# Moving half of a query load to ScalarE's DMA queue, and hanging the first weight loads on a sine

## Chip, cores, metric

One core of a Trainium2 chip. Its engines are TensorE (matmuls), VectorE, ScalarE (tables such as sine and Gelu), GpSimd and SyncE; the last three also issue the DMA transfers here, each into a queue of its own. "Cast" is a copy to another number type, and the granted clock is the share of its full clock that TensorE was given. L372 is line 372 of a kernel's file. The metric is the device time of one execution in microseconds (us), median over runs. All runs told here are "fast": none is over 1.5% above the fastest of its kernel. A time is some 2 us longer than the span of the profile of the same execution, which runs from the first to the last instruction.

## The reference

Linear attention with position weights, then a gated feed-forward block over the tokens. q, k and v are (8 batches, 8 heads, 576 positions, 64), all float32.

```python
theta = np.pi / 2.0 * pos / S
phi = lambda x: concat([relu(x) * cos(theta), relu(x) * sin(theta)])   # last axis
q_p, k_p = phi(q), phi(k)
kv  = einsum('bhsf,bhsd->bhfd', k_p, v);  z = sum(k_p, axis=2)
num = einsum('bhsf,bhfd->bhsd', q_p, kv); den = einsum('bhsf,bhf->bhs', q_p, z)[..., None] + 1e-6
x = (num / den) as (4608, 512)
out = (gelu(x @ w_gate) * (x @ w_val)) @ w_out                         # 512 -> 1536 -> 512
```

## The kernel before

It is already tuned: the attention of batch b+1 is spread between the feed-forward matmuls of batch b, and TensorE is rarely idle. Only the first 20 us are a bare start-up. The parts concerned (cuts marked):

```python
wg_sb = weights.tile([128, CT, J], BF16)
wv_sb = weights.tile([128, CT, J], BF16)
# ...
load(nc.sync, "k", 0, 0, 2)              # SyncE's queue, in this order: k(0) first half
load(nc.sync, "k", 0, 2, 4)              # k(0) second half
load(nc.sync, "q", 0, 0, NP, 0, JA)      # q(0), positions j 0..3
load(nc.sync, "v", 0, 0, 2)              # v(0) first half
load(nc.sync, "v", 0, 2, 4)              # v(0) second half
load(nc.sync, "q", 0, 0, NP, JA, R)      # q(0), positions j 4..8
# ... position tables on ScalarE
nc.scalar.activation(sin_t, pos_f, AF.Sin, scale=th_scale)
nc.scalar.activation(cos_t, pos_f, AF.Sin, scale=-th_scale, bias=half_pi)
warm = consts.tile([128, 1], FP32)
nc.scalar.activation(warm, half_pi, AF.Gelu)          # fetches the Gelu table early
# ...
gate = consts.tile([128, 1], FP32)
gate2 = consts.tile([128, 1], FP32)
# ... k's sines on ScalarE (and GpSimd), cosines on VectorE
prep("k", 0, 1, range(R), 2, 4, nc.scalar)            # nine sines on k's second half
# ...
nc.gpsimd.tensor_copy(gate, staged["v", 0][:, 0, 0:1])  # GpSimd waits for v(0) first half
load_w(0, 2)                                            # then issues W: w_gate and w_val, 256 columns each
load_w(2, 2)
# ...
dummies(22)                                             # matmuls that only warm TensorE's clock
sines(0, 1, 2, 3)                                       # q's sines on ScalarE
turn_j(0, 0, 2, (0, 1), 0, act_copy)                    # transposes of q on TensorE
cast_v(0, 2, 4, dve_copy)                               # VectorE casts v's second half
turn_j(0, 2, 4, (0, 1), 1, dve_copy)
kv_pairs(0, 0, 2, (6, 7))                               # the small matmuls k x v
# ...
kv_pairs(0, 2, 4, (4, 5))
# ...
prep("q", 0, 0, (4, 5))                                 # first use of q(0), positions 4..8
```

## Time and profile before

| | before |
|---|---|
| time, median | 326.56 us (3 runs); 326.49 with the three runs made later beside the changed kernel, which lie between 325.86 and 327.50 |
| profiled span | 323.9 us |
| v's second half: cast starts | 10.76 us |
| the last 32 matmuls of the first feed-forward pieces (L372) start | 19.49 us |

The prediction shows the chain and the traffic of the start.

### The profile page before, as it was taken

What the parts mean: (1) busy time and instruction counts of PE and PEld (TensorE: products, weight loads), DVE (VectorE), ACT (ScalarE), POOL (GpSimd) and SP (SyncE); (2) the same over time, 40 slices, a digit from 0 to 9 for tenths busy, and PEclk for the clock granted to TensorE, in tenths of its full rate; (3) what the DMA queues carried; (4) which work ended last, traced back from release to release, by engine and by line L of the source; (5) the groups of instructions that cost most, each with busy time, mean ns of one, the idle gap of its engine ahead of it and who ended that gap; (6) DMA issues with size and microseconds to landing.
All of it is one profiled execution on the core that took longest, in us unless ns stands there. A gap on an engine that the chain in (4) does not pass through costs nothing.

```text
span 323.9 us, 6340 instructions
## 1 busy us (share of the span) xinstructions
PE 316.8 (98%) x2451; PEld 164.5 (51%) x2451; DVE 170.3 (53%) x407; ACT 159.3 (49%) x336; POOL 26.0 (8%) x43
## 2 busy tenths in 40 slices
PE   8899999999999999999999999999999999999995
PEld 3574556555754564545544554445544444444443
DVE  5854677759665952793586348544532222222211
ACT  7864858946466832673457336633222332222220
POOL 6684410000000000000000000000000000000000
PEclk9999999999999999999999999999999999999999
DMA  7999999842999689938957990543431111111124
GB/s 274 249 186 273 297 352 366 230 111 51 323 216 354 166 147 383 201 83 251 330 96 157 383 232 1 137 102 78 85 73 33 34 32 32 35 32 32 34 65 98
DMA packets 69102, 53.57 MB, mean 165 GB/s; under 512 B 45392, under 2 KB 54352, under 8 KB 69072
## 3 DMA queue, kind: packets, MB, share of 16 engines
q1 hardware_dynamic: 59264, 41.23, 48.1%
q0 software_dynamic: 9648, 11.80, 15.7%
q8 instruction: 19, 0.31, 0.4%
q10 hardware_dynamic: 160, 0.13, 0.1%
q14 instruction: 11, 0.09, 0.1%
HBM read 37.75 MB, written 9.44 MB: 146 GB/s over the span
## 4 chain that ended last, share of the span: by engine, by line
PE 93%; DMA 2%; DVE 2%; SPq 1%; issue 0%; DVEq 0%
PE ps L400 57%; PE ps L430 28%; PE ps L282 3%; PE ps L241 3%; DMA vf<-in_v_dram 2%; PE ps L204 1%; PE ps L372 1%; PE ps L697 1%; SPq L80 1%; PE ps L357 0%; DVE qp L162 0%; DVE x_sb L322 0%; DVE vx L179 0%; DVE x_sb L295 0%; DVE qT L486 0%
## 5 line engine op out<-in xcount | busy, mean ns | idle before, releaser
L409 DVE TENSOR_TENSOR hT<-gel,ps 128x512 bf16<-128x512 f32 (+1 forms) x114 | 74.1, 650 | 128.9 <-PE ps L400 126.0
L408 ACT ACTIVATE gel<-ps 128x512 f32<-128x512 f32 (+1 forms) x114 | 64.8, 569 | 109.7 <-PE ps L400 108.0
L400 PE MATMUL ps<-xT,wv_sb 128*128 128x512 bf16 (+1 forms) x456 | 110.2, 364 | 0.0
L400 PE MATMUL ps<-xT,wg_sb 128*128 128x512 bf16 (+1 forms) x456 | 110.2, 364 | 0.0
L430 PE MATMUL ps<-wo_sb,hT 128*128 128x512 bf16 x420 | 105.8, 379 | 0.0
L400 PEld LDWEIGHTS <-wv_sb 128*128 128x128 bf16 x456 | 44.6, 98 | 47.0
L400 PEld LDWEIGHTS <-wg_sb 128*128 128x128 bf16 x456 | 44.0, 98 | 46.1
L430 PEld LDWEIGHTS <-hT 128*128 128x128 bf16 x420 | 38.3, 98 | 39.4
L439 ACT COPY o_sb<-ps 128x512 f32<-128x512 f32 x34 | 19.9, 587 | 29.9 <-PE ps L430 27.6
L160 ACT ACTIVATE qp<-qf,sin_t 128x256 bf16<-128x256 f32 x72 | 32.0, 501 | 0.4 <-DMA qf<-in_q_dram 0.4
L160 ACT ACTIVATE kp<-kf,sin_t 128x256 bf16<-128x256 f32 (+1 forms) x73 | 29.9, 479 | 0.9 <-DMA kf<-in_k_dram 0.9
L295 DVE TENSOR_TENSOR x_sb<-ps,rec 128x512 bf16<-128x512 f32 x38 | 26.3, 691 | 1.3
L162 DVE TENSOR_SCALAR qp<-qf,cos_t 128x256 bf16<-128x256 f32 x71 | 21.8, 353 | 2.3 <-DMA qf<-in_q_dram 2.3
L282 PEld LDWEIGHTS <-qT 128*128 128x128 bf16 x304 | 14.6, 98 | 7.9 <-ACT qT L486 0.3
L162 DVE TENSOR_SCALAR kp<-kf,cos_t 128x256 bf16<-128x256 f32 x63 | 18.3, 349 | 0.0
L282 PE MATMUL ps<-kv_sb,qT 128*128 128x65 bf16 x304 | 16.0, 194 | 0.0
L179 DVE CAST vx<-vf 128x1152 bf16<-128x1152 f32 (+1 forms) x15 | 12.0, 804 | 0.8 <-DMA vf<-in_v_dram 0.8
L250 ACT CAST kv_sb<-ps 128x260 bf16<-128x260 f32 x14 | 4.6, 383 | 12.9 <-PE ps L241 12.9
L241 PEld LDWEIGHTS <-kp 64*128 64x128 bf16 x504 | 8.5, 95 | 3.0 <-issue 3.0
L140 PE MATMUL ps<-dummy 128*128 128x512 bf16 x27 | 8.4, 457 | 1.5 <-POOL dummy L113 1.5
L241 PE MATMUL ps<-vx,kp 64*128 64x65 bf16 x504 | 9.3, 191 | 0.0
L294 DVE RECIPROCAL rec<-den 128x8 f32<-128x8 f32 x38 | 7.7, 203 | 1.3
(60 smaller groups left out, 100.6 us busy)
## 6 DMA issues: line engine op xcount, KB each, us to landing
out_dram<-o_sb SPq DMA_DIRECT2D x70, 128.0 KB, 2.6
kf<-in_k_dram SPq DMA_DIRECT2D x12, 576.0 KB, 6.2
vf<-in_v_dram SPq DMA_DIRECT2D x12, 576.0 KB, 8.3
qf<-in_q_dram SPq DMA_DIRECT2D x10, 576.0 KB, 5.0
qf<-in_q_dram POOLq DMA_DIRECT2D x4, 576.0 KB, 12.2
kf<-in_k_dram POOLq DMA_DIRECT2D x4, 576.0 KB, 12.5
vf<-in_v_dram POOLq DMA_DIRECT2D x4, 576.0 KB, 12.8
wg_sb<-in_moe_w_gate_dram POOLq DMA_DIRECT2D x6, 256.0 KB, 6.4
```

What stands on the lines that cost most here:

```text
L140: nc.tensor.matmul(bank(to), lhsT=dummy[:, 0:128], rhs=dummy, start=True, stop=True)
L160: nc.scalar.activation(o, i, AF.Relu, scale=tab[:, j:j + 1])
L162: (eng or nc.vector).tensor_scalar(o, i, 0.0, tab[:, j:j + 1], op0=ALU.max, op1=ALU.mult)
L179: copy(vx_tiles[b % 2][:, m0:m1, j0:j1, 0:D], staged["v", b][:, m0:m1, j0 * D:j1 * D].rearrange("p m (j d) -> p m j d", d=D),)
L241: nc.tensor.matmul(bank(6 + i)[:, m * (D + 1):(m + 1) * (D + 1)], lhsT=kp[rr, m, j, :], rhs=vx[rr, m, j, :], start=(j == 0), stop=(j == R ...
L282: nc.tensor.matmul(bank(b0 + h // 4)[:, (h % 4) * (D + 1):(h % 4 + 1) * (D + 1)], lhsT=q_cols(b, t, h), rhs=kv_sb[b][:, h // 2, h % 2, :], ...
L295: nc.vector.tensor_tensor(x, nm[:, :, :, 0:D], rec[:, :, :, None].to_broadcast([128, 2, 4, D]), op=ALU.mult,)
L400: nc.tensor.matmul(bank(b0 + g)[:, 0:w], lhsT=wt[:, ct, js], rhs=xt[:, ct, c0:c0 + w], start=(ct == 0), stop=(ct == CT - 1),)
L408: nc.scalar.activation(gel[:, 0:w], bank(b0)[:, 0:w], AF.Gelu)
L409: nc.vector.tensor_mul(hT[n][:, jt, c0:c0 + w], gel[:, 0:w], bank(b0 + 1)[:, 0:w])
L430: nc.tensor.matmul(bank(to), lhsT=hT[n][:, jt, tt * 128:(tt + 1) * 128], rhs=wo_sb[:, jt, :], start=(jt == 0), stop=(jt == JT - 1),)
L439: copy(o_sb, bank(to))
```

## The change

The intent, as far as the code tells it: SyncE's queue is relieved of its last transfer, which ScalarE issues instead, and W starts earlier. W's gate is no longer v's arrival. The sine table is written a second time into the place where W's own buffer will lie; the seventh of the nine k sines (GATE = 6) reads its factor from there, and so W's first transfer, which overwrites it, must wait for that sine and for nothing else.

```diff
+    GATE = 6
-    wg_sb = weights.tile([128, CT, J], BF16)
+    early = weights.tile([128, CT * J // 2], FP32, name="wg_sb")
 ...
-    load(nc.sync, "q", 0, 0, NP, JA, R)
 ...
     nc.scalar.activation(sin_t, pos_f, AF.Sin, scale=th_scale)
+    nc.scalar.activation(early[:, 0:R], pos_f, AF.Sin, scale=th_scale)
     nc.scalar.activation(cos_t, pos_f, AF.Sin, scale=-th_scale, bias=half_pi)
     warm = consts.tile([128, 1], FP32)
+    load(nc.scalar, "q", 0, 0, NP, JA, R)
 ...
     gate = consts.tile([128, 1], FP32)
-    gate2 = consts.tile([128, 1], FP32)
 ...
-                nc.scalar.activation(o, i, AF.Relu, scale=tab[:, j:j + 1])
+                t = early if (name, b, m0, j) == ("k", 0, 2, GATE) else tab
+                nc.scalar.activation(o, i, AF.Relu, scale=t[:, j:j + 1])
 ...
-    nc.gpsimd.tensor_copy(gate, staged["v", 0][:, 0, 0:1])
+    wg.append(weights.tile([128, CT, J], BF16, name="wg_sb"))
     load_w(0, 2)
     load_w(2, 2)
-    nc.gpsimd.tensor_copy(gate2, wg_sb[:, 0, 0:1])
+    nc.gpsimd.tensor_copy(gate, wg[0][:, 0, 0:1])
     load_w(4, 2)
-    nc.gpsimd.tensor_copy(gate2, wv_sb[:, 0, 0:1])
+    nc.gpsimd.tensor_copy(gate, wv_sb[:, 0, 0:1])
 ... (wg_sb becomes wg[0] where it is read)
```

`gate2` goes, since one small tile now serves both copies.

More of the change, by code (lines that the diff above doesn't have):

```diff
@@ L90 @@
     wo_r = moe_w_out.rearrange("(jt p) c -> p jt c", p=128)
+    wg = []
     def load_w(jt0, n):
         sl = slice(jt0 * 128, (jt0 + n) * 128)
-        nc.gpsimd.dma_start(out=wg_sb[:, :, sl], in_=wg_r[:, :, sl])
+        nc.gpsimd.dma_start(out=wg[0][:, :, sl], in_=wg_r[:, :, sl])
         nc.gpsimd.dma_start(out=wv_sb[:, :, sl], in_=wv_r[:, :, sl])
@@ L367, in gv_tile @@
     def gv_tile(t):
-        for g, wt in ((0, wg_sb), (1, wv_sb)):
+        for g, wt in ((0, wg[0]), (1, wv_sb)):
             for jt in range(2):
@@ L397, in gv_unit @@
             hT[n] = ffn.tile([128, JT, BLK], BF16, name="hT")
-        for g, wt in ((0, wg_sb), (1, wv_sb)):
+        for g, wt in ((0, wg[0]), (1, wv_sb)):
             for ct in range(CT):
```

## The prediction

> **What bounds the kernel now.** I read the page's totals first, then the chain that ended last, then the first 32 us engine by engine, and last the DMA traffic of that stretch in slices of one microsecond.
>
> ```profile
> span 323.9 us, 6340 instructions
> PE 316.8 (98%) x2451; PEld 164.5 (51%) x2451; DVE 170.3 (53%) x407; ACT 159.3 (49%) x336; POOL 26.0 (8%) x43
> PE 93%; DMA 2%; DVE 2%; SPq 1%; issue 0%; DVEq 0%
> ```
>
> TensorE carries 93% of the chain. What isn't TensorE, 7% or some 20 us, must sit where TensorE waits, and the chain of waits told in order of time says where: its first 19 us.
>
> ```profile
> 2.27 0.51 SPq L80
> 2.78 0.04 issue
> 2.82 7.92 DMA vf<-in_v_dram
> 10.74 0.02 issue
> 10.76 0.86 DVE vx L179
> 11.62 0.65 DVE qT L486 x2
> ...
> 12.48 0.29 DVE kv_sb L230
> 12.78 0.63 DVE qp L162 x2
> ...
> 13.95 1.29 DVE x_sb L322 x2
> 15.24 0.79 DVE qp L162 x2
> ...
> 19.49 1.79 PE ps L372 x32
> 21.27 6.91 PE ps L400 x32
> ```
>
> The columns are start, length, what. The second half of v(0), the fifth transfer of SyncE's queue, lands at 10.74; VectorE casts it, and from there VectorE and TensorE hand over to each other without a pause to the dense matmuls at 19.5. After that the chain is matmuls to the end, so a shift of the start is carried whole. Note that q(0)'s second part isn't on this chain: its first use is the VectorE step at 12.78, which starts when the step before it ends. It was issued at 3.39 and took 9.0 us to land (the view of that tile gives 6.1 us for the first part and 9.0 for the second), so it is there at 12.4, 0.4 us early.
>
> Why does v land at 10.74? Each slice of these lines gives busy microseconds of the engines, then granted clock, DMA share, GB/s:
>
> ```profile
> 1.00:2.00 1.00, 0.47 (x2) 0.20 (x3) 0.93 (x3) 1.00 (x1) 0.93 (x5) 1.00 0.11 21
> ...
> 4.00:5.00 1.00, 1.00 (x4) 0.38 (x3) 0.46 (x1) 0.48 (x3) 0.38 (x1) 1.00 1.05 406
> ...
> 9.00:10.00 1.00, 0.77 (x8) 0.49 (x8) 0.85 (x2) 1.00 (x4) 0.60 (x1) 1.00 1.02 393
> 10.00:11.00 1.00, 0.84 (x40) 0.76 (x40) 0.37 (x2) 0.67 (x2) 1.00 (x2) 1.00 1.07 398
> 11.00:12.00 1.00, 0.82 (x29) 0.73 (x29) 1.00 (x3) 0.69 (x2) 1.00 (x3) 1.00 0.51 169
> ```
>
> From 2 to 11 us the 16 DMA engines are full. The start is bound by bandwidth, and what counts is the order in which bytes come: k, k, q first part, v, v, and only then q second part, which is needed last. In the trace's packet records a half of k or v is 256 packets of 2304 B (16 per DMA engine, 93 ns each: 1.49 us), q's first part 512 of 1024 B (32 x 46 ns = 1.47 us), its second 512 of 1280 B (32 x 55 ns = 1.76 us). Data start at 1.95. I take 1.1 times the running sum for the slowest engine and 0.6 us to the landing, both fitted by me: 4.2, 5.8, 7.5, 9.1, 10.7, 12.7, where the trace has 4.4, 5.85, 7.9, 9.4, 10.7, 12.4.
>
> W isn't short: its first two pieces land at 14.2 (issued at 10.11, 4.1 us) and 16.5 (11.06 + 5.4), and the matmuls that read them run from 16.48 and 16.93 behind other matmuls, without an idle gap put down to a W transfer.
>
> **What the Trainium skill says.** "DMA: Bandwidth & Descriptors", section "Issuing engines are not separate DMA queues": transfers started from different engines end on the same 16 DMA engines and interleave, so issuing from a second engine saves only sequencer time. Same page, "Queues, rings and completion order": each DMA engine goes round robin over the queues that have work. The trace before agrees with the first as far as it can (one queue fills all 16 engines, share 1.02 to 1.07); it has no long overlap of two hardware queues, so the sharing itself is not yet shown here. "TensorE: Matmul & The Clock Gate", section on the warm-up: an idle window of about 3.4 us halves the clock. Before, TensorE's longest gap after the warm-up matmuls is 0.87 us and the clock row shows 9s throughout.
>
> **The change, part by part.**
> (1) It takes the sixth transfer from SyncE's queue. SyncE had issued it at 3.39 behind everything, so v is issued no earlier: gain 0.
> (2) ScalarE gets one 128x9 sine (starts are 0.12 us apart in the pair there now) and the issue (0.48 us on SyncE) ahead of the second table load. The issue starts at 2.50 + 0.12 = 2.62, the table load at 3.1 instead of 2.51, the warm Gelu ends at about 4.6 instead of 4.0, and the first k sine starts at 4.7 instead of 4.52. The wait of 0.36 us before the second half's sines swallows that: cost 0.
> (3) q's second part now flows beside k, q and v. SyncE's first data came 1.2 us after its issue began, so q's second part starts at 3.85, when three of the second k half's 16 packets are through. Packet for packet, 13 rounds of 93 + 55 ns, x1.1, are 2.1 us: that half ends at 5.97 and lands at 6.6 (5.85 before). q's remaining 19 packets pass with 19 of the first part: 19 x 101 ns x 1.1 = 2.1, to 8.1, landing at 8.7, four microseconds earlier than anyone can use it. The rest of q's first part: 13 x 46 x 1.1 = 0.66, landing at 9.35 (7.9). Then v: 11.0 (9.4) and 12.6 (10.74). The debt of 1.76 us x 1.1 has moved from the unneeded end of the queue to in front of v.
> (4) W's gate. Before, GpSimd waited for v's first half, spent 0.77 us on a copy and issued W at 10.11. Now it waits for the seventh of nine sines on the second k half. Nine took 2.74 us, so starts are 0.294 apart: 6.6 + 6 x 0.294 + 0.39 = 8.75. W is issued 1.3 us earlier. Its packets came 1.5 us after the issue and in strength after 2.4, so now at 10.3 and 11.2, in the last microsecond of v's second half. Some ten of v's 16 packets then alternate with a W packet (22.7 per engine and us in the slices where W is alone: 44 ns): +0.45 us, so v lands at 13.0.
> (5) Behind it nothing gets shorter. ScalarE's q sines run 9.35 to 11.05 (8.52 to 10.2), v's first cast ends at 11.8, the first half's 36 small matmuls and their copies are ready before 13.0. From the cast of the second half on, VectorE runs the same list. W's lead lies where TensorE doesn't wait for W.
> Sum: 13.0 - 10.74 = +2.3 us on 326.56: 328.9.
>
> **Rivals.**
> (a) v isn't delayed: the second queue's packets come later or get a smaller share, or its traffic fits beside SyncE's. For it: where W runs alone the DMA share is 1.3 to 1.46, so an engine can overlap packets. Against it: 400 GB/s in the slices already, W's own slices move no more (about 186 GB/s written, from twice as many bytes read), and q's part would have to be served behind v's, though it is issued before v's second half (2.62 against 2.82). Time then: 326 to 327.
> (b) Earlier W is worth something, or TensorE stalls on W less further on. For it: the first W pieces land only 0.4 us before their use. Against: between 19.5 and 34 us the chain is matmuls back to back. At most 0.5 us: 326.0.
> (c) TensorE cools. Its 22 warm-up matmuls end at 8.2 as before, the first transpose moves from 9.06 to about 10, and until 13.9 it is mostly idle. If the clock gate closes, the small matmuls up to the dense stage take twice their time, +1 to 2 us on top: 330 to 331. Against: no single gap reaches 3.4 us.
> (d) The packets are shared by whole transfers and not one by one: the second k half lands on time, W is issued at 8.1 and meets all of v. v lands at 13.3 to 13.7: 329.3.
>
> **Range and chances.** I give the delay (3 to 5, with d) three chances in four at 1.5 to 3 us, and a and b a quarter at -0.5 to +0.8. Weighted, the centre is a little below the sum: 328.5. Eight in ten: 326.5 to 330.3. Two per cent are 6.5 us; no part of the start that changes is long enough for a gain of that size (0.5%), and a loss would need c to come on top of everything (2%).
>
> **What would show it.** Step 3: q's second part lands near 8.7 from ScalarE's queue, q's first part after 9, v's halves near 11 and 13, with the DMA still at about 400 GB/s from 3 to 12 us. Step 4: GpSimd's first W issue at 8.1 to 8.8. Step 5: VectorE's second cast starts at 12.5 to 13.5, and the dense matmuls start about 2.3 us later than 19.49, with the spans differing by as much. Step 2: k's first sine within 0.3 us of 4.52. It is wrong if the second cast starts before 11.5; if it does start late but the dense matmuls don't, something behind the cast had slack that I didn't see. A clock row with digits below 9 in the first slices would mean c.

## More of the kernel before

One more row of the page is needed later: TensorE's granted clock, in tenths, in 40 slices of 8 us.

```profile
PEclk9999999999999999999999999999999999999999
```

## The result

The changed kernel took 329.23 us (median of 6 runs, 329.03 to 329.95), before 326.49: 1.0085 times as long, 95% interval 1.0066 to 1.0104. Every ratio here is the mean time of one kernel's fast runs over that of the other's of the same rounds, so it isn't quite the ratio of the medians. Later (experiment e6) the same changed kernel gave 328.24 and 1.0044 (1.0019 to 1.0070). So the loss is 1.3 to 2.7 us, under 1%, and how large it comes out differs between executions. The experiments show why.

The page of the changed kernel: the span and the clock row.

```profile
span 328.0 us, 6302 instructions
PEclk9789999999999999999999999999999999999999
```

The clock row, all nines before, has a 7 and an 8 in its second and third slice. Next, ScalarE's timeline (start, length, what, and in brackets the idle time before it with what ended it):

```profile
2.10 0.51 ACTq L81 DMA_DIRECT2D qf<-in_q_dram  x1
...
4.58 0.99 ACT L166 ACTIVATE kp<-kf,sin_t 128x128 bf16<-128x128 f32 x3 [0.44 <-DMA kf<-in_k_dram]
6.00 1.86 ACT L166 ACTIVATE kp<-kf,sin_t 128x128 bf16<-128x128 f32 x6 [0.43 <-DMA kf<-in_k_dram]
...
9.56 1.71 ACT L166 ACTIVATE qp<-qf,sin_t 128x256 bf16<-128x256 f32 x4 [0.83 <-DMA qf<-in_q_dram]
```

The issue goes out at 2.10, beside the sines and not behind them. k arrives almost as before (4.58 and 6.00, against 4.52 and 5.87), but the first part of q is waited for until 9.56 (8.52 before). GpSimd's and VectorE's timelines, the line of W's first issue and those of v's two casts:

```profile
8.46 0.96 POOL L99 DMA_DIRECT2D wg_sb<-in_moe_w_gate_dram  x1 [0.50 <-ACT kp L166]
```

```profile
11.53 0.77 DVE L185 CAST vx<-vf 128x1152 bf16<-128x1152 f32 x1 [0.45 <-DMA vf<-in_v_dram]
13.02 0.76 DVE L185 CAST vx<-vf 128x1152 bf16<-128x1152 f32 x1 [0.73 <-DMA vf<-in_v_dram]
```

W goes out at 8.46 instead of 10.11, and v's second half is cast at 13.02 instead of 10.76: +2.26 us. The chain of waits shows that this isn't all:

```profile
2.27 9.23 DMA vf<-in_v_dram
11.50 0.02 issue
11.53 0.78 DVE vx L185
12.30 0.05 issue
12.35 1.17 PE ps L224 x33
13.52 0.97 PE ps L210 x8
14.48 1.10 PE ps L224 x36
15.59 0.54 PE ps L145
16.13 0.88 PE ps L313 x16
...
23.38 1.79 PE ps L378 x32
```

The matmuls that began at 19.49 begin at 23.38, 3.9 us later. In between, the chain before ran over VectorE; now it runs over TensorE, whose 36 small matmuls take 1.1 us where they took 0.75. TensorE is slow there. Its windows (length, busy us of PE with the number of instructions, granted clock, DMA share, GB/s):

```profile
8.12:11.53 3.41, 0.79 (x8) 1.00 1.07 385
11.53:18.36 6.83, 5.79 (x106) 0.50 1.42 201
```

From 11.53 to 18.36 the clock was halved. If v's 2.26 us are taken off the 3.89, 1.63 are left for the clock. That is a subtraction, not yet shown: the chain above goes through v's first half (cast at 11.53, 9.37 before) and then stays on the slow TensorE. e4 below tests it. After that matmul for matmul the distance to before stays at +3.89 up to 75 us and +4.07 from there to the end.

Two questions: what delays v, the second queue or the earlier W? And how much of the time is the clock's, which isn't in the code at all?

### The profile page after: what moved, and what is told of

It is laid out like the page before. It is cut to its first block, busy times and chain, and to the rows that moved or that the text cites. A ratio compares the mean times of both kernels' runs of the same rounds, so it can differ in the third digit from the quotient of the medians.

```text
span 328.0 us, 6302 instructions
## 1 busy us (share of the span) xinstructions
PE 316.0 (96%) x2414; PEld 166.4 (51%) x2451; DVE 170.5 (52%) x407; ACT 159.6 (49%) x337; POOL 25.2 (8%) x42
## 4 chain that ended last, share of the span: by engine, by line
PE 93%; DMA 3%; issue 1%; DVE 1%; SPq 0%; ACT 0%; DVEq 0%
PE ps L406 56%; PE ps L436 27%; PE ps L288 3%; DMA vf<-in_v_dram 3%; PE ps L247 3%; PE ps L210 1%; PE ps L378 1%; PE ps L703 1%; PE ps L224 1%; PE ps L363 1%; SPq L81 0%; ACT qT L492 0%; PE ps L313 0%; DVE vx L185 0%; DVE x_sb L301 0%
## 5 line engine op out<-in xcount | busy, mean ns | idle before, releaser
L436 PE MATMUL ps<-wo_sb,hT 128*128 128x512 bf16 x401 | 103.0, 379 | 1.4 <-issue 0.8
L185 DVE CAST vx<-vf 128x1152 bf16<-128x1152 f32 (+1 forms) x15 | 11.9, 797 | 1.2 <-DMA vf<-in_v_dram 1.2
L210 PE MATMUL ps<-ident,qp 128*128 128x128 bf16 x72 | 6.5, 240 | 2.5 <-ACT qp L166 2.3
## 6 DMA issues: line engine op xcount, KB each, us to landing
kf<-in_k_dram POOLq DMA_DIRECT2D x4, 576.0 KB, 13.1
```

The source lines that it names most:

```text
L185: copy(vx_tiles[b % 2][:, m0:m1, j0:j1, 0:D], staged["v", b][:, m0:m1, j0 * D:j1 * D].rearrange("p m (j d) -> p m j d", d=D),)
L210: nc.tensor.transpose(out=dst[:, n * 128:(n + 1) * 128], in_=phi["q", b][:, m, j, :], identity=ident,)
L436: nc.tensor.matmul(bank(to), lhsT=hT[n][:, jt, tt * 128:(tt + 1) * 128], rhs=wo_sb[:, jt, :], start=(jt == 0), stop=(jt == JT - 1),)
```

## The experiments

Twelve runs, all correct, each with five rounds; e6 and e8 repeat the two kernels and e7 repeats e4. Times are compared with the kernel before.

| kernel | median (before) | ratio, 95% | span | v's second cast | clock halved for | L372 group | q(2) transposed lands after |
|---|---|---|---|---|---|---|---|
| before | 326.49 | | 323.9 | 10.76 | 0 | 19.49 | 5.4 |
| changed | 329.23 (326.49) | 1.0085 (1.0066 to 1.0104) | 328.0 | 13.02 | 6.83 | 23.38 | 6.8 |
| e1 q alone | 328.70 (327.01) | 1.0056 (1.0036 to 1.0077) | 326.4 | 12.33 | 3.41 | 21.89 | 5.6 |
| e2 gate alone | 327.07 (327.01) | 1.0006 (0.9982 to 1.0029) | 325.3 | 12.11 | 0 | 20.57 | 6.5 |
| e3 q late | 328.31 (327.01) | 1.0043 (1.0021 to 1.0064) | 326.7 | 12.23 | 3.41 | 21.86 | 6.8 |
| e4 changed, warm | 329.55 (327.01) | 1.0077 (1.0055 to 1.0099) | 327.6 | 13.15 | 0 | 21.55 | 7.5 |
| e5 q last | 327.12 (326.92) | 1.0002 (0.9986 to 1.0017) | 325.2 | 11.29 | 3.41 | 20.76 | 5.6 |
| e6 changed again | 328.24 (326.92) | 1.0044 (1.0019 to 1.0070) | 325.1 | 12.28 | 0 | 20.68 | 6.6 |
| e7 changed, warm again | 329.62 (326.92) | 1.0081 (1.0066 to 1.0097) | 327.1 | 12.84 | 0 | 21.24 | 7.0 |
| e8 before again | 326.92 (326.92) | 0.9996 (0.9979 to 1.0013) | 325.0 | 11.02 | 3.41 | 20.54 | 5.5 |
| e9 changed, aligned | 328.31 (326.91) | 1.0045 (1.0020 to 1.0070) | 325.7 | 12.71 | 0 | 21.23 | 5.6 |
| e10 before, shifted | 326.97 (326.91) | 1.0017 (0.9992 to 1.0041) | 326.6 | 11.58 | 3.41 | 21.01 | 6.9 |
| e11 changed, warm, aligned | 327.57 (326.91) | 1.0025 (1.0005 to 1.0045) | 325.4 | 12.38 | 0 | 20.91 | 5.6 |
| e12 before, warm | 326.86 (326.91) | 1.0002 (0.9980 to 1.0024) | 325.1 | 11.55 | 0 | 20.65 | 5.7 |

The last five columns come from the one profiled execution of each, in us; the last is the median from issue to landing of the two DMA transposes of q(2) at 60 to 70 us. How far two executions differ is to be seen in the rows of before and e8, and of changed and e6. The first profile of before is one of its shortest executions: 323.9 us, where the spans of its 39 executions in the later calls go from 323.6 to 325.7. So distances to that profile come out long. In the four profiles with the transfers in the order and on the queue of before (before, e8, e10, e12) v's second cast starts at 10.76 to 11.58, mean 11.23; in the six with the changed order (changed, e4, e6, e7, e9, e11) at 12.28 to 13.15, mean 12.73. That is 1.5 us later, not 2.26.

The record also gives the mean granted clock of the unprofiled executions (of before's not in the first call). It is 0.990 to 0.995 in the profiles with a halved stretch and 0.998 to 1.000 in those without, and the other executions fall into the same two groups (0.995 or less, 0.997 or more). I take the low group for executions with a halved stretch:

| | clock not halved: runs, mean time | halved: runs, mean time |
|---|---|---|
| changed | 0 | 6, 329.31 |
| e6, changed again | 4, 327.85 | 2, 329.73 |
| e9, changed, aligned | 3, 327.53 | 3, 329.07 |
| e1, q alone | 1, 328.48 | 5, 328.63 |
| before, e1's call | 10, 326.71 | 1, 327.71 |
| before, e6's call | 10, 326.98 | 1, 327.30 |
| before, e9's call | 8, 326.63 | 3, 327.19 |

So with an open clock the change costs some 0.9 us in the seven such executions that there are (327.85 against 326.98, 327.53 against 326.63; e1's only one lies higher, 328.48 against 326.71), and where the clock closes in the changed kernel another 1.5 to 1.9. It closed in all six executions of the first call, in 5 of the 12 of e6 and e9, and in 7 of before's 39.

### e1: the transfer alone

```diff
 # on the kernel before
-    load(nc.sync, "q", 0, 0, NP, JA, R)
 ...
     warm = consts.tile([128, 1], FP32)
+    load(nc.scalar, "q", 0, 0, NP, JA, R)
```

> The kernel before with q(0)'s second part issued by ScalarE behind the two table sines, W gated on v's first half as before. Theory A (q's second part is served ahead of v, the W gate matters little): v's second half still lands late, its cast starts at 12.3 to 12.8 (10.76 before, 13.02 in the changed kernel; the missing 0.3 to 0.5 is W's share), and the time is 2 to 2.7 us above before, 328.5 to 329.2. Rival B (the earlier W transfers take the bandwidth from v): the cast starts before 11.3 and the time is within 0.7 us of before. If TensorE's clock closes here too (gap from 8.0 to about 10.1, then little work), 1 to 1.6 us of the loss are the clock's.

Measured: the cast starts at 12.33 and the time is 1.0056 times that of before.

```profile
12.33 0.87 DVE L179 CAST vx<-vf 128x1152 bf16<-128x1152 f32 x1 [0.62 <-DMA vf<-in_v_dram]
```

GpSimd issued W only at 11.69 here, and no W packet moved before 13 us, so W has no part in it. Theory A holds: the moved transfer alone makes the kernel slower, by 1.7 us, most of the loss (five of the six executions had a halved clock). v is cast 1.57 us later than in the first profile of before. Some 0.6 of that isn't the transfer's: ScalarE had its first k at 5.12 here (4.52 before), and the first moved packet came only at 6.23. The packet records show how the rest comes about. From 7.0 to 8.0 us 143 packets of 1280 B (ScalarE's queue) started beside 149 of SyncE's: nearly one for one.

### e2: the gate alone

```diff
 # on the changed kernel
     load(nc.sync, "v", 0, 2, 4)
+    load(nc.sync, "q", 0, 0, NP, JA, R)
 ...
-    load(nc.scalar, "q", 0, 0, NP, JA, R)
```

> The changed kernel with q(0)'s second part back as SyncE's last transfer; only W's gate is changed. W is issued at about 8.4 instead of 10.1, its packets come from about 10. Theory A: v's second half is met only at its end, the cast starts at 10.9 to 11.4, q's second part lands at 12.8 to 13.4 and its VectorE step (12.78 before) waits for it; time +0.2 to +0.8 us. Rival B: the cast starts after 12 and the time is 2 us or more above before.

Measured: 1.0006, so the time doesn't change beyond noise, and rival B's 2 us are excluded. The profile is less tidy: the cast starts at 12.11, later than the 10.9 to 11.4 expected. But the first part of q was waited for until 9.04 already (8.09 before), two microseconds before the first W packet at 11.2: in this execution the last packet of that part started at 8.55 (7.53 before). One profile doesn't separate W's share from that; the five rounds say it is within -0.6 and +1.0 us.

### e3 and e5: when is a transfer on the second queue served?

In the changed kernel the moved transfer was issued at 2.10, but its first packet came at 5.97, where I had 3.85. e3 issues it later, e5 much later.

```diff
 # e3, on the changed kernel
-    load(nc.scalar, "q", 0, 0, NP, JA, R)          # behind the table sines
 ...
-    prep("k", 0, 1, range(3), 0, 2, nc.scalar)
+    prep("k", 0, 1, range(1), 0, 2, nc.scalar)
+    load(nc.scalar, "q", 0, 0, NP, JA, R)
+    prep("k", 0, 1, range(1, 3), 0, 2, nc.scalar)
```

> The changed kernel, but ScalarE issues q(0)'s second part behind its first k sine (at about 4.6, when SyncE has issued everything). In the changed kernel the part's packets began only at 6.2, 4.1 us after the issue at 2.10. In-order theory (what is issued first is served first, whichever queue): packets begin when v's are nearly through, 9 or later, v's second half lands at 10.8 to 11.4, time within 0.8 us of before. Round-robin theory with a start latency of 1.2 us as on SyncE: packets begin at 5.8, the result is that of the changed kernel, 329.2. A fixed latency of 4.1 us on ScalarE's queue: packets begin at 8.7, cast at about 12, time +1 to +2.

Measured: issued at 4.43, first packet at 8.37, v's second cast at 12.23, 1.0043. That is nearest to "a fixed latency of 4.1 us" (8.7, cast at 12), and I had to test that against another reading: 8.37 is also where v's second half, the last thing SyncE had issued, began (first packets at 8.3 in before). The loss is in the size expected for the fixed latency, but here v's first half wasn't touched (cast at 9.88), only the second.

```diff
 # e5, on e1
-    load(nc.scalar, "q", 0, 0, NP, JA, R)          # behind the table sines
 ...
-    sines(0, 1, 2, 3)
+    sines(0)
+    load(nc.scalar, "q", 0, 0, NP, JA, R)
+    sines(1, 2, 3)
```

> The kernel before (W gated on v), with q(0)'s second part issued by ScalarE behind its first q sine, at about 8.2. So far that part's first packet came 3.7 to 4.1 us after its issue on ScalarE (2.10 to 5.97, 2.10 to 6.23, 4.43 to 8.37), where SyncE's first transfer took 1.1. Theory F (a latency of some 4 us on ScalarE's queue): first packet at about 12.2, landing at about 14.5, its VectorE step (12.78 before) waits 1.5 to 2 us, time +1.5 to +2. Theory G (an issue waits until the descriptors of everything issued before it are out; v's second half, the last of them, had its first packet at 8.3): first packet 1 to 1.5 us after the issue, 9.2 to 9.7, landing at about 12.5 to 13, v's second half cast at 10.8 to 11.2; time within 0.7 us of before. Either way v is hardly delayed, and the clock stays at 1.0.

ScalarE's timeline of e5:

```profile
8.39 0.44 ACTq L80 DMA_DIRECT2D qf<-in_q_dram  x1
```

First packet at 9.62, 1.2 us after the issue, and the part landed 4.7 us after it, at 13.1; its VectorE step began at 13.92, behind others. So the latency isn't fixed, theory F falls. What all four cases fit is theory G: a transfer's packets start 1.1 to 1.2 us after its issue if all transfers issued ahead of it have begun (SyncE's first: 0.74 to 1.84), and else not before those, on either queue, have begun (issued 2.10 between q's first part and v: 5.97, where those began at 5.14 and 6.68; issued at 4.43 behind all: 8.37). From then on the two queues alternate. G is an inference from start times; no run looks into the DMA engines. The time of e5 is that of before (1.0002): with the same queue, but issued behind v, the move costs nothing that these runs can see (interval -0.0014 to +0.0017). v's second cast is at 11.29, within the spread of kernels that don't move the transfer (10.76 to 11.58). My expectation that the clock would stay open failed; it was halved for 3.41 us.

### e4 and e7: keeping TensorE warm

```diff
 # on the changed kernel
-    dummies(22)
+    dummies(31)
 ...
+    dummies(5)
     kv_pairs(0, 0, 2, (6, 7))
```

> The changed kernel with 9 more warm-up matmuls behind the 22 (they fill 8.0 to 10.0) and 5 more in the wait for v's first half (11.1 to 12.2). In the changed kernel's profile the granted clock was 0.5 from 11.6 to 18.4 us, and the dense stage started 3.9 us later though v came 2.26 later. Theory: the clock stays at 1.0 in all slices, the cast still starts at about 13.0, the dense matmuls (19.49 before, 23.38 changed) start at about 21.8, the profiled span is about 1.6 us below the changed kernel's 328.0, and the median 0.4 to 1.6 us below 329.2, depending on how often the clock closes unprofiled. Rival: the gap between 2.26 and 3.9 is other waiting; then neither moves.

The clock was 1.0 throughout, v's second cast at 13.15, and the L372 group began at 21.55, 2.06 us after that of before where v came 2.39 later. So the theory of the start holds: with v as late as in the changed kernel, 1.8 of the 3.9 us went with the halved clock. But the span was 327.6 and not 326.4, and the median was not lower: 329.55. Matmul for matmul, of the 1.8 us won in the start against the changed kernel 1.6 were lost again at one place, 75 us. The chain of waits of e4 there:

```profile
67.22 8.51 DMA qT<-qp
75.72 0.05 issue
75.77 0.40 PE ps L288 x7
```

TensorE waits for the DMA transpose of q(2), issued at 67.22. That wait isn't in before. I repeated the pair, changed and changed-warm, on one chip:

> The changed kernel once more, beside the next run on the same chip: +2.2 to +3.3 us on before as at first; in the profile the clock at 0.5 for 3.4 or 6.8 us somewhere between 11 and 19 us, and v's second cast at 12.7 to 13.2.

> The changed kernel kept warm (9 + 5 more warm-up matmuls), once more, now beside the changed kernel on the same chip. If the clock closes in most executions of the changed kernel, this one is 0.7 to 1.6 us faster than it. If it closes only in some (the profiled ones), the two are within 0.4 us. Profile: clock 1.0 throughout, start of the dense matmuls 2.1 us after that of before; whether the wait of 1.4 us at 75 us for the transposed q(2) comes again tells whether it belongs to this kernel or to that execution.

e6 came out at +1.3 us, below what I expected (+2.2 to +3.3), and its clock didn't close: v's cast at 12.28, L372 at 20.68, 1.2 us after before, span 325.1. Its six times run from 327.06 (that profile) to 330.03. e7 was slower than e6, not faster, and lost 1.44 us at 75 us again. So neither branch of e7's expectation held: the wait at 75 us belongs to the kernel, and it hides what a warm clock is worth.

### e8: before, twice

> The kernel before itself, to see how far two executions of one kernel differ: time ratio 1.000 within 0.002. The clock stays at 1.0; v's second cast at 10.7 to 11.3; if the times of before are of two kinds (325.8 to 326.2 and 327.0 to 327.7 so far), the profile of one of the slower kind shows where the extra microsecond is: in the start, or at 75 us in the wait for the transposed q(2).

Ratio 0.9996, as it must be. But the clock didn't stay at 1.0 as I expected. The window before the closing in e8, and the one at the same place in before (same columns as above):

```profile
8.03:11.44 3.41, 1.86 (x51) 1.00 1.03 386
```

```profile
8.52:11.94 3.42, 2.36 (x69) 1.00 0.90 337
```

In e8 the clock was halved from 11.44 to 14.85 and the start took 1.05 us longer; v came only 0.26 later. The stretches of the clock are multiples of 3.41 us and lie differently against the program in each execution. Windows are counted here in steps of 3.41 us from the edges of these stretches. TensorE was busy 1.86 us of the window in e8, after which the clock closed, and 2.36 in the first profile, after which it didn't. In all the profiles the windows of the start that turned an open clock into a halved one held 0.79 (changed), 0.99 (e1), 1.04 (e10), 1.32 (e5), 1.69 (e3) and 1.86 us (e8) of work.

The sum of work doesn't sort them from the others: the clock stayed open after 1.91 us in e9 (10.73 to 14.14) and after 1.67 us in e11 (319.83 to 323.24, near the end). It nearly does if TensorE's transposes, matmuls with the identity matrix `ident`, are left out: the six windows then held 0 (changed), 0.20 (e1), 0.25 (e10), 0.52 (e5), 0.76 (e8) and 1.00 us (e3), the last window of an execution, after which the clock closes too, at most 1.07 (e10), and every window that left the clock open 1.01 (before) or more. This is read from 14 profiles in which the ends of matmuls are modelled, and no run tests it.

So the start of before is at the edge already, and the change, which thins out TensorE's work between 8 and 13 us, pushes it over more often and for longer.

### e9, e10, e11: 32 bytes

What do e4 and e7 have that makes the transposes late? Their DMA packets were slow, and not only theirs. The average of 256-byte packets between 60 and 70 us was 30 or 31 ns in changed, e2, e3, e4, e6 and e7, and 17 or 18 in before, e5 and e8. It was 28 in e1, and 26 in the later e12, whose transposes land nearly as fast as those of before, so the average of these 10 us isn't a sure sign. That of the whole execution is: 20.9 to 22.3 ns in all kernels with `gate2`, e1 and e12 among them, and 29.1 to 30.0 in all without. 4608-byte packets between 50 and 60 us took 193 to 195 ns in the first six, and 179 or 180 in the others, e1 among them. The six slow kernels are those without `gate2`. The built programs have it in their addresses: without that tile all large tiles lie 32 bytes lower, the transposed q at 138208 instead of 138240, a multiple of 256.

```diff
 # e9, on the changed kernel; e11 the same on e4
     gate = consts.tile([128, 1], FP32)
+    nc.gpsimd.memset(gate, 0.0)
+    gate2 = consts.tile([128, 1], FP32)
 ... (the two later copies write gate2)
 # e10, on the kernel before
-    gate2 = consts.tile([128, 1], FP32)
 ... (the copies write gate)
```

> The changed kernel with the removed 128x1 tile put back (one memset of 128x1 on GpSimd is added, so that both small tiles exist). Without it every large tile of the changed kernel lies 32 bytes lower, at an odd multiple of 32 (qT at 138208 instead of 138240). In all six profiles of kernels without that tile, 256-byte packets between 60 and 70 us took 28 to 31 ns on average and 4608-byte ones at 50 to 60 us 193 to 195; in the three profiles with it and the first part of the change undone or absent 17 to 18 and 179 to 180. Theory (the address of the tiles makes the packets slow): 17 to 20 ns and 179 to 180 here. Rival (the earlier W or the order of the transfers makes them slow): 28 to 31 and 193 as in the changed kernel. The time hardly tells: 327.5 to 329.3, v's second cast at 12.2 to 13.0.

> The kernel before with its second 128x1 tile dropped (one tile serves all copies), nothing else: all large tiles 32 bytes lower. Theory: 256-byte packets between 60 and 70 us at 28 to 31 ns instead of 17, 4608-byte ones at 193 instead of 180; the transposed q(2) has about 1 us less in hand, time 0 to +1.0 us. Rival: 17 and 180 as before, time unchanged.

> The changed kernel, kept warm and with the tiles back at their old addresses. Both profiles of the warm one lost another 1.4 to 1.6 us at 75 us, waiting for the transposed q(2). If that is the slow packets' doing, this one keeps its start (+1.5 to +2.1 us on before) to the end: profiled span 325.4 to 326.1, time 0.8 to 1.6 us below the 329.6 of the warm one. If not, span 327 or more and time 329 or more.

Measured, 256-byte and 4608-byte packets: 17 and 178 ns in e9, 17 and 178 in e11, and 30 and 194 in e10. One small tile does it, in both directions (e9 and e11 add a memset of that tile, e10 adds nothing). That it is the distance to a multiple of 256, and not some other effect of the 32 bytes, no run shows. The landing of the transposes, before and e10:

```profile
DMA to landing us min/median/max: 5.4/5.4/5.4
```

```profile
DMA to landing us min/median/max: 6.5/6.9/7.3
```

That is 1.1 to 1.9 us taken from a wait that had little in hand. In e11 it is 5.6, the wait at 75 us is gone, and the distance to before stays +1.42 from 20 us to the end: span 325.4, time 327.57, 1.0025. Against the warm kernel without the tile (e7, 329.62) that is 2.05 us, more than the 0.8 to 1.6 I expected, on different chips with equal medians of before (326.92 and 326.91). In the changed kernel itself the place at 75 us cost only 0.17 us in one profile and nothing in the other, where TensorE came to it at another time; why the warm kernels have the least in hand there I haven't settled. e10's own time (1.0017, interval across 1) shows no sure loss for before; its profile has another late transfer, a load of q at 52 us, which cost 0.86 us there.

e9 against e11 is what the clock costs with the addresses right: 328.31 against 327.57. e9's six times are of two kinds, 327.42 to 327.63 (its profile is one of these, with the clock at 1.0) and 328.98 to 329.25; e11's run from 327.29 to 327.98. No profile fell into the slow kind of e9, but the clocks do tell: 0.997 to 0.999 in the three fast executions, 0.990 to 0.995 in the three slow ones. So the slow kind is the one with the halved clock.

### e12: would a warm start help the kernel before?

```diff
 # on the kernel before
-    dummies(22)
+    dummies(26)
 ...
+    dummies(1)
     kv_pairs(0, 0, 2, (6, 7))
 ...
+    dummies(1)
     kv_pairs(0, 2, 4, (4, 5))
```

> The kernel before with four more warm-up matmuls (26) and one more ahead of each of the first two groups of small matmuls, where TensorE waits for v. Of two profiles of before, one had the clock at 0.5 for 3.4 us from 11.4 and was 1.05 us longer. Theory (some executions of before are slower because the clock closes there): the clock is 1.0 throughout and the median falls by 0.3 to 0.9 us, to 326.0 to 326.6, with fewer runs above 327. Rival (the two kinds of times have another cause): unchanged within 0.2, or a little slower because the extra matmuls delay the small ones.

The clock stayed at 1.0, the time didn't move (1.0002). Three of its runs lie at 326.2 to 326.5 and three at 327.3 to 327.5, all six with a mean clock of 0.998 or more, so the two kinds of times have at least one more cause. In the profiled execution, one of the slower, v came late (11.55), and TensorE stood 0.3 us for the second W piece. The profiles of before and of the changed kernel don't have that wait. It is the only sign that W's start isn't free of stakes, as rival (b) had it. Against e12, with both kernels warm and at the same addresses, e11 is 0.7 us slower (327.57 and 326.86): about what an open clock left of the change above. No run of the twelve beats before.

## Why the prediction was right

It said 328.5 us, with 326.5 to 330.3; measured were 329.23 and, again, 328.24. The sign and the number were right, and the cause it named, the moved transfer, does start the loss (e1, e5). But the number was right partly by luck: the sum has 2.3 us from v's delay alone, and in the seven executions of the changed order with an open clock the change cost 0.9. The rest of the measured 2.7 came with the halved clock, which the sum leaves out. Not every step was right either.

1. The removal gains nothing: right. e5, which removes the transfer from SyncE's queue too, has the time of before.
2. ScalarE's extra work costs nothing: right. The first k sine began at 4.58 (4.52 before). I had the issue at 2.62, behind the sines; it went out at 2.10.
3. The transfer takes bandwidth ahead of v: right in kind, shown by e1 alone and by e5, in which the same transfer behind v costs nothing. Packets do alternate, 143 against 149 in e1. Wrong was where it begins: 5.97 instead of 3.85. So k's second half wasn't delayed (6.00, not 6.6) and the part landed near 11.9 (issue 2.10 plus 9.8), not 8.7. v's second cast was at 13.02 in the profile, 13.0 predicted, and 12.28 in the second one. Over all profiles v is 1.5 us late and not 2.26, so this term of the sum was too large.
4. W's gate: issued at 8.46, predicted 8.75, because k wasn't late. W's first packet came at 11.32, 2.9 us after its issue, and not at 10.3. The +0.45 us for W's packets in v's tail were not confirmed: e2 has +0.2 us, with an interval from -0.6 to +1.0.
5. Nothing behind v gets shorter: right for the other engines. With a clear clock the start of the dense stage follows v within some tenths (e11: v +1.62, L372 +1.42).
6. Rival (c), TensorE cools, I kept out of the sum because no gap reaches 3.4 us. That was the wrong test. The longest gap was 2.13 us, and the clock closed all the same, after a window with 0.79 us of work. All of that work was transposes: without them TensorE had nothing from 8.00 to 12.35. In the first profile this was some 1.6 us, as (c) said, and where it is absent the loss is smaller than my sum: +1.2 us in e6's start, 0.9 us in the times. So (c) did come, in all six executions of the first call, on top of a delay that by those seven executions costs less than half of the sum.
7. What I didn't see at all is the 32 bytes: I read the removal of `gate2` as tidying.
8. The centre: three quarters of 1.5 to 3 us and a quarter of -0.5 to +0.8 make +1.7 us, 328.3 and not the 328.5 that I gave.

## What to carry to other kernels

When the DMA engines are full, a second queue gives no bandwidth (from 3 to 11 us 369 GB/s in the changed kernel and 387 in e1, 388 before): it only decides whose bytes pass first, so issue what is needed last behind what is needed first, whichever engine issues it. Compare the addresses of the large tiles before and after any change that adds or drops a small one. And a start-up with thin work on TensorE should be judged by several executions, for one profile may show a halved clock and the next not.

## What the Trainium skill lacked or had wrong

- "DMA: Bandwidth & Descriptors", section "Latency and other measured facts", gives some 0.6 us to the first byte for transfers from SyncE and ScalarE, and not from where it counts. From the end of the issuing instruction the runs are near it: 0.6 us for SyncE's first transfer (1.21 to 1.84), 0.8 in e5 (8.83 to 9.62). From its start it was 1.1 and 1.2. With transfers issued ahead on the other queue that hadn't begun it was 3.9 (2.10 to 5.97 and 4.43 to 8.37), and the page gives no such wait.
- "TensorE: Matmul & The Clock Gate", section "Part 1: The HAM clock gate", has the clock close after an idle window of about 3.4 us. The window's length agrees (3.41 and 6.83 us stretches), but it needn't be idle: windows with 0.76 us (e8) and 1.00 us (e3) of TensorE work besides transposes were followed by a halved clock. The section also tells of a kernel whose clock goes to and fro with short pauses, but gives no amount of work that keeps it open; here the line, as far as 14 profiles show it, lies near 1 us without transposes (closed after at most 1.07, open after at least 1.01).
- "DMA: Bandwidth & Descriptors", section "How a descriptor splits into AXI transactions", says that a descriptor that starts off a 256-byte boundary has its first transaction begin at the boundary below, so that unused bytes are fetched too. The runs fit that, without showing that it is the reason, and give a size: 32 bytes lower, 256-byte packets of the DMA transposes went from 21.4 to 29.3 ns over the whole execution (before and e10) and 4608-byte ones from 180 to 194 at 50 to 60 us. It lacks the warning that the size of a small tile elsewhere moves all large tiles off that boundary.
